# Attention and experts in one kernel: the last batch gated as a whole, gate weights and w1 in part on GpSimd, two ranks' rows in one product

## The chip, the cores and the metric

One core of a Trainium2 chip runs the kernel. The metric is the device time of one execution in microseconds, lower is better; the time before is a median of three runs, 620.59 us (620.38 to 622.92).

## The reference

Eight batches of 576 tokens go through attention with eight heads of 64 (four with a local mask of 32 positions, four with a strided one). The result, 4608 tokens of 512 values, goes through a layer of eight experts: each token is sent to the one expert with the largest logit.

```python
def _moe_ref(x, w_gate, w_output_gate, w1, w2):
    logits = x @ w_gate                                  # 4608 x 8
    e_idx = np.argmax(logits, axis=1)
    probs = softmax(logits); gate_w = probs[np.arange(N), e_idx]
    eom = 1.0 / (1.0 + np.exp(-(x @ w_output_gate)))
    for e in range(E):
        mask = e_idx == e
        h = np.maximum(x[mask] @ w1[e], 0.0)             # 512 -> 1024
        ye = h @ w2[e]                                   # 1024 -> 512
        out[mask] = gate_w[mask, None] * eom[mask, e, None] * ye
```

## The kernel before

**Order.** Both halves of the kernel stand under a manual schedule: each engine executes its instructions in the order in which the program writes them, and waits only for data. So the order of the Python calls is the order of every queue.

**Attention** (line 173) walks over 40 steps, five per batch, with the stages of several steps interleaved. Beside them run generators, the chains: each `pump()` advances those that are due, and a `yield n` puts a chain off by n pumps. A chain `logits` (line 409) computes the logits of half a batch: eight products on TensorE, a copy to `lg` on ScalarE, three turns (transposes) on TensorE, a sum on VectorE; then it goes on into `gating` (line 539). After step 40 a second loop drains the pipeline; from its fourth pass on it only pumps chains and calls `fill`.

**Gating** of n blocks of 96 tokens: one-hot `oh` of the chosen expert (VectorE), `numbers` (TensorE: running number of each token in its expert, from the counts `cum` so far), `slots` (VectorE), then `hit`, which compares the slot's low and high part with constant rows, and `named`, five products of the high part with the token's number (two) and with three bf16 parts of its gate weight (`parted`). `place(v0, v1)` (line 658) multiplies `hit` and `named` of all blocks held on TensorE and `enter` adds the result to `book`, which lists for every expert its tokens and weights. Batches 0 to 6 are gated whole (HALVED = 7); batch 7 in two halves of three blocks, its numbers going through `cum` one after the other. For the very last half `place(0, 2)` comes first, so that `tokens_first` can work out `idx0`, the rows of the leading expert; `weights`, `parted` and the other three `named` follow on VectorE, then `count` and `place(2, 5)`.

**Fillers.** The expert with the most tokens in the first four batches leads (rank 0). Its first 256 rows go through the first layer while attention still runs: `lead_layer` (line 500) yields one product at a time, 32 in all, and `fill(n)` (line 746) issues n of them, two instructions each. Eight products make a pair of columns j; the four pairs alternate between two PSUM banks of `acc`. When a pair is finished, `flush` evacuates it: `hha` by a ScalarE activation, then `hla` by a VectorE operation (lines 509, 510). While `hold[0]` is set a finished pair stays, until a later call finds `hold` cleared, or its bank is wanted two pairs later:

```python
if done and (not hold[0] or (i == c == 0 and done[0][0].start < j - 2)):
    flush(j)
```

**Experts** (line 1222). float32 operands are split into a high and a low part (`split`, line 973: a ScalarE cast, then a VectorE subtraction), and each product is three products (`w1h xh`, `w1h xl`, `w1l xh`). Rank 0 first finishes layer 2 for its first 256 rows: two groups of 24 products (`by_token`), the second interleaved with turning rank 0's other 480 rows and splitting w1. Then for each rank r: eight times `layer1(r, j)`, then `layer2`, which is interleaved with turns and splits for rank r + 1. Capacities are fixed per rank, `CAPS = (736, 704, 672, 640, 608, 576, 544, 512)`. `halves(r)` gives layer 1 one product, if at most 512 rows are left, or else two: 256 rows from `xs[0]` and the rest from `xs[1]`, into one of four PSUM banks `hps` in turn (`rotate`). The last product's width depends on the data: `choose` branches on TensorE by the spare of the rank (capacity minus tokens) and takes n - 24 a columns, a = 0 to 3. `arms(r)` (line 1216) loads the spare into a register of TensorE. `copied` (line 964), called after `layer1(0, 1)`, makes twelve small products of `pages` into `hps[3]`.

Of the kernel before, what the change touches and what calls it, by code (L numbers as in the profile page):

```python
# [35 lines left out]
HALVED = B - 1  # L36
# [5 lines left out]
FD = (0, 1, 1)  # L42
PN = 4
LF = (5, 7)
# [16 lines left out]
def attn_moe_kernel(  # L61
# [111 lines left out]
    def attention():  # L173
        with ExitStack() as actx:
# [234 lines left out]
            def logits(b, hf):  # L409
# [129 lines left out]
            def gating(b, j0, j1, ci):  # L539
                n = j1 - j0  # L540
                steady = ci < HALVED - 1
# [34 lines left out]

                def sigmoid():
                    nc.scalar.activation(out=f[:, 4, :], in_=f[:, 3, :], func=AF.Exp, scale=-1.0)
# [25 lines left out]
                else:  # L604
# [8 lines left out]
                    exp_sum()  # L613
                    yield 0
                V.tensor_tensor(out=cum[0:QB, ci + 1, :], in0=cum[0:QB, ci, :], in1=s8, op=ALU.add)  # L615
                yield 0 if steady else 1
                dst = slots[:, tcols]
                V.tensor_tensor(out=dd[:, 3], in0=pv.rearrange("p (j e) -> p j e", j=n), in1=oh, op=ALU.mult)
                yield 0
                with nc.allow_low_precision(reason="one slot's number among zeros, written as an integer"):  # L620
                    R(out=dst, in_=dd[:, 3], axis=AX.X, op=ALU.add)
                yield 0
# [10 lines left out]
                P, last = nc.gpsimd, ci == NC - 2  # L633
# [12 lines left out]
                def parted():  # L646
                    left = wall[:, tcols]
                    for i in range(WP):
                        W.tensor_copy(out=parts[:, i, :], in_=left)
                        if i + 1 < WP:  # L650
                            W.tensor_tensor(out=rest[:, i, :], in0=left, in1=parts[:, i, :], op=ALU.subtract)
# [6 lines left out]
                def place(v0, v1):  # L658
                    wp = ps_g.tile([128, 512], F32, name="gp")[:, 0:(v1 - v0) * nh]
                    blocks = [(h[:, j, 0:128], m[:, j, v0:v1, :]) for h, m, k in held for j in range(k)]  # L660
                    for i, (h, m) in enumerate(blocks):
                        nc.tensor.matmul(out=wp, lhsT=h, rhs=m.rearrange("p v s -> p (v s)"),
                                         start=(i == 0), stop=(i == len(blocks) - 1))
                    return wp

                def enter(wp, v0, v1):
                    flat = book[:, v0:v1].rearrange("p v e k -> p (v e k)")
                    if ci:
                        V.tensor_tensor(out=flat, in0=flat, in1=wp, op=ALU.add)
                    else:  # L670
                        V.tensor_copy(out=flat, in_=wp)

                if ci == HALVED - 1:
                    yield 4
# [29 lines left out]
                else:  # L704
# [3 lines left out]
                    if held and not last:  # L708
                        wp = place(0, 2 + WP)
                        held.clear()  # L710
                        yield 1
                        enter(wp, 0, 2 + WP)
# [9 lines left out]
                    else:  # L722
                        hold[0] = True
                        fill(LF[0])
                        wp = place(0, 2)
                        enter(wp, 0, 2)
# [5 lines left out]
                        parted()  # L732
                        for v in range(2, 2 + WP):
                            name(v)
# [130 lines left out]
            while t < ns + 4 or chains or fillers:  # L865
# [20 lines left out]
                fill(FT[0][k] if k < 4 else FD[0])  # L886
# [566 lines left out]
```

## Time and profile before

| | |
|---|---|
| median of three runs | 620.59 us |
| the profiled execution | 622.88 us |
| its span, first to last instruction | 621.1 us |
| TensorE busy | 582.6 us (94%) |
| VectorE, ScalarE, GpSimd busy | 317.8, 281.1, 198.5 us |
| granted TensorE clock, mean | 0.991 |

The page cuts the span into 40 slices of 15.5 us; attention fills roughly the first eleven, the experts the rest. The timeline lists instructions in order of time with start and length, equal neighbours merged, and in brackets the idle time of the engine before them and what ended it. Ends of matmuls are modelled, and a matmul's length is longer than the distance to the next one; the distance of two starts is what a matmul costs in a row of them.

### The profile page before, as it was taken

The numbers are of one execution on the slowest core, as the hardware profiler recorded it, in microseconds if no ns is written. First come the engines' busy times: TensorE is split into PE (matmuls) and PEld (weight loads), VectorE is DVE, ScalarE is ACT, GpSimd is POOL, SyncE is SP. The second block draws the span as 40 slices with busy tenths as digits, with TensorE's granted clock in tenths as the row PEclk, the third lists the DMA queues.
The fourth block names the chain that finished last, engine by engine and source line by source line (L and its number), as shares of the span: only waits on it lengthen the run. The fifth ranks groups of instructions, "written<-read, shape, count | busy, mean of one in ns | idle before, by whom it ended". The sixth has DMA issues, their size and how long they took to land. (4 is left out here: it accounts for less than half of the span.)

```text
span 621.1 us, 14987 instructions
## 1 busy us (share of the span) xinstructions
PE 582.6 (94%) x5863; PEld 499.6 (80%) x5863; DVE 317.8 (51%) x746; ACT 281.1 (45%) x567; POOL 198.5 (32%) x285
## 2 busy tenths in 40 slices
PE   7799999988979999999999999999999999999990
PEld 5676677766657989988998899889889989988880
DVE  4888888997788353432343234235434433542400
ACT  3788777766344253333332334334334434443310
POOL 3337767666333225021401130223034034011030
PEclk9999999999999999999999999999999999999996
DMA  9898898894524755053306330642165165060010
GB/s 316 294 315 288 295 289 284 292 301 138 181 63 147 278 165 159 2 193 134 121 2 204 130 109 2 195 156 80 49 200 158 27 219 154 32 237 34 3 43 17
DMA packets 42489, 97.95 MB, mean 158 GB/s; under 512 B 5458, under 2 KB 16346, under 8 KB 42394
## 3 DMA queue, kind: packets, MB, share of 16 engines
q1 hardware_dynamic: 34122, 73.47, 36.3%
q0 software_dynamic: 6864, 19.74, 9.7%
q10 hardware_dynamic: 1408, 3.38, 1.5%
q8 instruction: 72, 1.18, 0.8%
q14 instruction: 23, 0.19, 0.1%
HBM read 77.74 MB, written 20.58 MB: 158 GB/s over the span
## 5 line engine op out<-in xcount | busy, mean ns | idle before, releaser
L1040 PE MATMUL hp<-xh,w1h 128*128 128x256 f32 (+2 forms) x448 | 138.2, 308 | 0.2 <-issue 0.2
L1040 PE MATMUL hp<-xl,w1h 128*128 128x256 f32 (+2 forms) x448 | 138.0, 308 | 0.1
L1040 PE MATMUL hp<-xh,w1l 128*128 128x256 f32 (+2 forms) x448 | 137.9, 308 | 0.0
L1040 PEld LDWEIGHTS hp<-xl,w1h 128*128 128x128 f32 x448 | 84.8, 189 | 1.5 <-DVE xl L975 0.4
L1040 PEld LDWEIGHTS hp<-xh,w1h 128*128 128x128 f32 x448 | 84.8, 189 | 1.5 <-DVE copies L971 0.3
L1040 PEld LDWEIGHTS hp<-xh,w1l 128*128 128x128 f32 x448 | 84.8, 189 | 0.5
L1153 POOL DMA_INDIRECT out_dram<-ys,idx x32 | 32.9, 1027 | 133.2 <-ACT ys L1152 128.8
L1055 DVE SCALAR_TENSOR_TENSOR hlb<-hp,hhb 128x384 fp32r<-128x384 f32 (+4 forms) x64 | 35.0, 549 | 78.6 <-ACT hf L1054 78.6
L1153 POOL DMA_INDIRECT out_dram<-ys,ri x18 | 20.0, 1113 | 172.2 <-ACT ys L1152 169.1
L1052 ACT ACTIVATE hhb<-hp 128x384 fp32r<-128x384 f32 (+4 forms) x64 | 31.0, 484 | 95.5 <-PE hp L1040 94.0
L1066 PE MATMUL yp<-w2h,hhb 128*128 128x512 f32 (+1 forms) x176 | 70.3, 400 | 0.0
L975 DVE TENSOR_TENSOR xl<-tp,xh 128x512 fp32r<-128x512 f32 (+3 forms) x40 | 25.8, 649 | 86.9 <-ACT xh L974 86.9
L1066 PE MATMUL yp<-w2l,hhb 128*128 128x512 f32 (+1 forms) x176 | 68.7, 391 | 0.0
L1066 PE MATMUL yp<-w2h,hlb 128*128 128x512 f32 (+1 forms) x176 | 68.6, 390 | 0.0
L974 ACT CAST xh<-tp 128x512 fp32r<-128x512 f32 (+3 forms) x40 | 22.0, 556 | 101.1 <-PE tp L1028 101.1
L309 POOL TENSOR_TENSOR p_t<-p_t,st 128x512 f32<-128x512 f32 x40 | 42.6, 1064 | 53.5 <-DVE cum L615 15.8
L158 POOL DMA_INDIRECT xg<-xd,idx x40 | 43.5, 1088 | 15.1 <-issue 8.2
L1066 PE MATMUL yp<-w2h,hha 128*128 128x512 f32 x112 | 45.3, 405 | 2.2 <-ACT w2h L974 1.6
L975 DVE TENSOR_TENSOR w1l<-raw,w1h 128x1024 fp32r<-128x1024 f32 x32 | 39.1, 1224 | 12.2 <-ACT w1h L974 12.0
L1152 ACT ACTIVATE ys<-yp,pages 128x512 f32<-128x512 f32 (+1 forms) x36 | 24.9, 693 | 45.0 <-issue 35.5
L1066 PE MATMUL yp<-w2l,hha 128*128 128x512 f32 x112 | 43.9, 392 | 0.5 <-DVE w2l L975 0.5
L1066 PE MATMUL yp<-w2h,hla 128*128 128x512 f32 x112 | 43.7, 390 | 0.0
(214 smaller groups left out, 1096.2 us busy)
## 6 DMA issues: line engine op xcount, KB each, us to landing
raw<-in_moe_w_dram SPq DMA_DIRECT2D x54, 512.0 KB
vst<-in_vs_dram SPq DMA_DIRECT2D x8, 780.0 KB
vlt<-in_vl_dram SPq DMA_DIRECT2D x16, 292.5 KB
q_t<-in_ql_dram SPq DMA_DIRECT2D x8, 576.0 KB
q_t<-in_qs_dram SPq DMA_DIRECT2D x7, 650.0 KB
xd<-x_t SPq DMA_DIRECT2D x80, 54.0 KB
xd<-x_t SPq DMA_DIRECT2D x16, 256.0 KB
raw<-in_moe_w_dram ACTq DMA_DIRECT2D x6, 512.0 KB
```

Source lines behind the costliest of these rows:

```text
L158: nc.gpsimd.indirect_dma_start(out=dst, out_offset=None, in_=src, in_offset=bass.IndirectOffsetOnAxis(ap=idx, axis=0), bounds_check=top, o ...
L309: nc.gpsimd.tensor_tensor(out=p_t, in0=p_t, in1=st, op=ALU.subtract)
L974: nc.scalar.copy(out=hi, in_=src)
L975: nc.vector.tensor_tensor(out=lo, in0=src, in1=f32(hi), op=ALU.subtract)
L1040: nc.tensor.matmul(out=hp[:, 0:n], lhsT=w[:, k, 128 * j:128 * (j + 1)], rhs=x[:, k, 0:n], start=first, stop=(k == KC - 1 and w is w1l))
L1052: nc.scalar.activation(out=hh[:, j, 0:s], in_=hp[:, 0:s], func=AF.Relu)
L1055: nc.vector.scalar_tensor_tensor(out=hl[:, j, 0:s], in0=hp[:, 0:s], scalar=0.0, in1=f32(hh[:, j, 0:s]), op0=ALU.max, op1=ALU.subtract)
L1066: nc.tensor.matmul(out=yp[0:m, :], lhsT=h[:, j, o:o + m], rhs=w[:, j, :], start=(j == 0 and q == 0), stop=(j == FC - 1 and q == 2))
L1152: nc.scalar.activation(out=ys[0:m, 0:n], in_=yp[0:m, 0:n], func=AF.Copy, scale=w[0:m, :])
L1153: i = nc.gpsimd.indirect_dma_start(out=out.rearrange("t (k d) -> (t k) d", k=k), out_offset=bass.IndirectOffsetOnAxis(ap=row, axis=0), in_ ...
```

## The change

- Batch 7 is gated as a whole, six blocks (HALVED = 8). The chain of its second half sets `hold` right after its logits and issues three fillers; four more come before `numbers`. Batch 6's placing moves behind `numbers`; the slots come next, and counts and the sum of exponentials later. `hold` is cleared after `count_on`. The drain loop issues no fillers while a chain runs; 4 + 11 stand around the two placings.
- `parted` of batch 7 runs on GpSimd, as that of the others did; its `named` stay on VectorE.
- In the drain loop's first four passes the norms come ahead of the three pumps, not between them.
- In `experts`, the four memsets of `hps` become ScalarE activations; `arms(0)` moves from between the two groups of layer 2 into the second, at j = 5; the low parts of w1's last two chunks are subtracted on GpSimd; `first_spare` writes its integer with one instruction fewer; `copied` is called after `layer1(0, 3)`.
- Ranks whose rows exceed 512 by at most 64 (5 and 6: 576 and 544) take their first 512 rows from `xs[1]` as one product, the others from `xs[0]`. If the spare covers those others, only the first product is issued, 576 - 24 a or 544 - 24 a columns wide.

```diff
-HALVED = B - 1
+HALVED = B
+STEADY = B - 2
-FD = (0, 1, 1)
-LF = (5, 7)
+LF = (4, 11, 4, 3)
@@ logits
+                if b == B - 1 and hf:
+                    hold[0] = True
+                    fill(LF[3])
                 yield 1
@@ gating
                     sigmoid()
+                    if last:
+                        fill(LF[2])
                     pv = numbers()
-                    counts()
+                    if last:
+                        before = place(0, 2 + WP)
+                        held.clear()
+                        own_number()
+                        slot()
+                    else:
+                        counts()
...
                         if i + 1 < WP:
-                            W.tensor_tensor(out=rest[:, i, :], in0=left, in1=parts[:, i, :], op=ALU.subtract)
+                            P.tensor_tensor(out=rest[:, i, :], in0=left, in1=parts[:, i, :], op=ALU.subtract)
...
-                    if held and not last:
-                        wp = place(0, 2 + WP)
-                        held.clear()
-                        yield 1
-                        enter(wp, 0, 2 + WP)
                     for v in range(2):
                         name(v)
...
-                        hold[0] = True
                         fill(LF[0])
                         wp = place(0, 2)
+                        enter(before, 0, 2 + WP)
+                        exp_sum()
                         enter(wp, 0, 2)
                         for _ in tokens_first(0, HB, idx0):
                             pass
-                        hold[0] = False
                         for _ in weights():
                             pass
                         parted()
+                        counts()
+                        count_on()
+                        hold[0] = False
                         for v in range(2, 2 + WP):
                             name(v)
                         fill(LF[1])
@@ drain loop
                 for part in range(3):
                     at(norm, 4, part)
-                    if k < PN:
-                        pump()
                 at(rows, 4)
+                for _ in range(3 if k < PN else 0):
+                    pump()
...
-                fill(FT[2][k] if k < 4 else FD[2])
+                fill(FT[2][k] if k < 4 else 0 if chains else 4)
@@ experts
+    def over(r):
+        return rows_of(r) - WXB if 0 < rows_of(r) - WXB <= 64 else 0
...
+    def layer1_over(r, j):
+        m, n = over(r), rows_of(r)
+        (hp, rest), (hh, hl) = (rotate(hps) for _ in range(2)), hs[1]
+        a0 = -(-m // STEP) - 1
+        def form(a):
+            if a == a0:
+                products(rest, xs[0], j, m)
+            products(hp, xs[1], j, WXB if a == a0 else n - STEP * a)
+        choose(arms(r), a0, a0 + ARMS, form)
+        nc.scalar.activation(out=hh[:, j, :], in_=hp, func=AF.Relu)
+        nc.scalar.activation(out=hf[:, j, 0:m], in_=rest[:, 0:m], func=AF.Relu)
+        nc.vector.scalar_tensor_tensor(out=hl[:, j, :], in0=hp, scalar=0.0, in1=f32(hh[:, j, :]), op0=ALU.max, op1=ALU.subtract)
...
         for hp in hps:
-            nc.vector.memset(hp[:, WB - STEP * (ARMS - 1):WXB], 0.0)
+            nc.scalar.activation(out=hp[:, WB - STEP * (ARMS - 1):WXB], func=AF.Copy, scale=0.0,
+                                 in_=ecst[:, 0, 0:1].to_broadcast([128, WXB - WB + STEP * (ARMS - 1)]))
...
-        arms(0)
         between = {j: [(turn, 0, c, m)] for j, (c, m) in zip(TURN_AT, blocks(0))}
+        between[5] = [(arms, 0)]
         for c in range(2, KC):
-            between[TURN_AT[c - 2]].append((split_w, 0, 1, c))
+            between[TURN_AT[c - 2]].append((split_w, 0, 1, c, nc.gpsimd))
...
                     count_spare()
                     send_away()
+                if r == 0 and j == 3:
                     copied()
```

## Rows read from the trace of the kernel before

**Rows 1.** The page's slices of the span: busy tenths of TensorE

```profile
PE   7799999988979999999999999999999999999990
```

**Rows 2.** Timeline of TensorE, 161 to 187 us: start, length, operation, idle time before

```profile
161.40 0.69 PE L416 MATMUL gp<-xt,wgt 128*32 128x288 f32 x8
...
171.94 0.29 PE L662 MATMUL gp<-named,hit 96*128 96x96 bf16 x3 [1.70 <-DVE named L656]
172.07 3.25 PE L525 MATMUL sp<-xe,raw 128*128 128x256 f32 x14
...
176.20 0.35 PE L662 MATMUL gp<-named,hit 96*128 96x144 bf16 x3 [0.66 <-DVE named L656]
...
179.51 0.50 PE L1066 MATMUL yp<-w2h,hha 128*128 128x512 f32 x1 [1.62 <-ACT w2h L974]
...
186.69 0.49 PE L1066 MATMUL yp<-w2h,hha 128*128 128x512 f32 x1 [0.60 <-DVE hp L1231]
```

**Rows 3.** Timeline of VectorE, 169 to 177 us, the last half batch

```profile
169.89 0.15 DVE L618 TENSOR_TENSOR dd<-gp,oh 96x24 f32<-96x24 f32 x1
...
171.37 0.52 DVE L656 TENSOR_TENSOR named<-hit,hcst 96x144 bf16<-96x144 bf16 x2
...
172.27 0.25 DVE L669 TENSOR_TENSOR book<-book,gp 128x96 f32<-128x96 f32 x1 [0.38 <-PE gp L662]
...
175.34 0.80 DVE L656 TENSOR_TENSOR named<-hit,parts 96x144 bf16<-96x144 bf16 x3
...
176.07 0.68 DVE L510 SCALAR_TENSOR_TENSOR hla<-sp,hha 128x512 fp32r<-128x512 f32 x1
```

**Rows 4.** Timeline of ScalarE at 173 us, the third pair of the lead layer

```profile
173.20 0.60 ACT L509 ACTIVATE hha<-sp 128x512 fp32r<-128x512 f32 x1 [5.20 <-PE sp L525]
```

**Rows 5.** Timeline of VectorE and GpSimd, batch 6 with its six blocks

```profile
156.51 0.95 DVE L706 TENSOR_TENSOR hit<-hcst,lo 96x768 bf16<-96x768 f32 x1
...
159.16 0.18 POOL L649 CAST parts<-wall 96x6 bf16<-96x6 f32 x1
...
160.20 0.19 POOL L649 CAST parts<-rest 96x6 bf16<-96x6 f32 x1
```

**Rows 6.** Timeline of TensorE and VectorE, layer 1 of rank 0

```profile
199.76 0.69 PE L970 MATMUL hp<-pages,ident 128*64 128x96 f32 x12 [0.63 <-DVE pages L959]
...
207.19 0.35 PE L1040 MATMUL hp<-xh,w1l 128*128 128x408 f32 x1
...
208.29 0.66 DVE L1055 SCALAR_TENSOR_TENSOR hlb<-hp,hhb 128x480 fp32r<-128x480 f32 x1 [1.56 <-ACT hf L1054]
```

**Rows 7.** Timeline of VectorE, TensorE and GpSimd, and from the page a GpSimd group

```profile
192.20 1.22 DVE L975 TENSOR_TENSOR w1l<-raw,w1h 128x1024 fp32r<-128x1024 f32 x1
...
196.57 0.34 PE L1040 MATMUL hp<-xh,w1l 128*128 128x408 f32 x1
...
170.56 0.59 POOL L649 CAST parts<-rest 96x3 bf16<-96x3 f32 x1
...
L309 POOL TENSOR_TENSOR p_t<-p_t,st 128x512 f32<-128x512 f32 x40 | 42.6, 1064 | 53.5 <-DVE cum L615 15.8 <-DVE st L294 13.7 <-DVE f L588 6.2
```

**Rows 8.** Line 1040 by form, ranks 5, 6, 7 (first, last start), and two products of 512

```profile
L1040 PE MATMUL hp<-xh,w1h x64: 273/280/283, 472.5 to 494.8; 128*128 128x256 f32 x32, 128*128 128x248 f32 x32
...
L1040 PE MATMUL hp<-xh,w1h x64: 272/278/287, 520.1 to 542.0; 128*128 128x256 f32 x32, 128*128 128x240 f32 x32
...
L1040 PE MATMUL hp<-xh,w1h x32: 357/362/363, 566.5 to 585.1; 128*128 128x440 f32 x32
...
470.50 0.39 PE L1066 MATMUL yp<-w2h,hhb 128*128 128x512 f32 x1
...
471.86 0.39 PE L1066 MATMUL yp<-w2h,hhb 128*128 128x512 f32 x1
```

**Rows 9.** Stretches at the end: busy of TensorE, its loads, VectorE, ScalarE, GpSimd; granted clock

```profile
606.00:610.00 4.00, 0.04 (x1) 0.00 (x0) 0.00 (x0) 0.69 (x1) 0.97 (x1) 1.00 0.17 66
610.00:612.00 2.00, 0.00 (x0) 0.00 (x0) 0.00 (x0) 0.00 (x0) 0.00 (x0) 0.52 0.00 0
```

More of the change, by code (lines that the diff above doesn't have):

```diff
@@ L575, in exp_sum, with count_on, own_number, slot @@
                     R(out=f[:, 2, :], in_=dd[:, 1], axis=AX.X, op=ALU.add)
+                last = ci == NC - 2
+                dst = slots[:, tcols]
+                def count_on():
+                    V.tensor_tensor(out=cum[0:QB, ci + 1, :], in0=cum[0:QB, ci, :], in1=s8, op=ALU.add)
+                def own_number():
+                    V.tensor_tensor(out=dd[:, 3], in0=pv.rearrange("p (j e) -> p j e", j=n), in1=oh, op=ALU.mult)
+                def slot():
+                    with nc.allow_low_precision(reason="one slot's number among zeros, written as an integer"):
+                        R(out=dst, in_=dd[:, 3], axis=AX.X, op=ALU.add)
+                def place(v0, v1):
+                    wp = ps_g.tile([128, 512], F32, name="gp")[:, 0:(v1 - v0) * E * HB]
+                    blocks = [(h[:, j, 0:128], m[:, j, v0:v1, :]) for h, m, k in held for j in range(k)]
+                    for i, (h, m) in enumerate(blocks):
+                        nc.tensor.matmul(out=wp, lhsT=h, rhs=m.rearrange("p v s -> p (v s)"),
+                                         start=(i == 0), stop=(i == len(blocks) - 1))
+                    return wp
+                def enter(wp, v0, v1):
+                    flat = book[:, v0:v1].rearrange("p v e k -> p (v e k)")
+                    if ci:
+                        V.tensor_tensor(out=flat, in0=flat, in1=wp, op=ALU.add)
+                    else:
+                        V.tensor_copy(out=flat, in_=wp)
                 def sigmoid():
@@ L609, in gating @@
                     sigmoid()
+                    if last:
+                        fill(LF[2])
                     pv = numbers()
-                    counts()
+                    if last:
[3 more added lines that the diff above has]
+                        slot()
+                    else:
+                        counts()
+                        yield 0
+                        exp_sum()
+                        yield 0
+                if not last:
+                    count_on()
+                    yield 0 if steady else 1
+                    own_number()
                     yield 0
-                    exp_sum()
+                    slot()
                     yield 0
[L615 to L622, printed above, removed]
                 def weights():
@@ L631, in weights @@
                     yield 0
-                P, last = nc.gpsimd, ci == NC - 2
+                P = nc.gpsimd
                 W = V if last else P
@@ L656, in name @@
                     W.tensor_tensor(out=named[:, :, v, :], in0=high, in1=wide(val, nh), op=ALU.mult)
[L658 to L673, printed above, removed]
+                if ci == STEADY:
                     yield 4
@@ L732, in gating @@
                         parted()
+                        counts()
+                        count_on()
+                        hold[0] = False
                         for v in range(2, 2 + WP):
@@ L986, in place @@
     def place(r, c):
+        if over(r):
+            return (1, 128 * c) if 128 * c < WXB else (0, 0)
         return (1, 128 * c) if alone(r) else (0, 128 * c) if 128 * c < EH else (1, 128 * c - EH)
@@ L1012, in gather, with split_w @@
             xgs[r, c] = xg
-    def split_w(r, which, c):
+    def split_w(r, which, c, eng=nc.vector):
         raw = raws[r, which, c]
         if which == 1:
-            split(w1h[:, c, :], w1l[:, c, :], raw)
+            split(w1h[:, c, :], w1l[:, c, :], raw, eng)
         else:
```

40 lines of the change are left out of this document (22 added, 18 removed).

## The prediction

> **What bounds the kernel now.** I read the page's slices first. TensorE is busy in nine tenths or more of nearly every slice; after the start it dips a little in the ninth and tenth, and most in the twelfth, 171 to 186 us [rows 1], where attention hands over to the experts. From there to the end it never rests, so behind it only work that leaves TensorE counts, and inside it the waits. The timeline of TensorE alone gives those waits [rows 2]: 1.70 us at 171.94 and 0.66 at 176.20 (it waits for VectorE's `named`), 1.62 at 179.51 (for the cast of w2 on ScalarE), 0.60 at 186.69. All four can be reached by this change. The run profiled took 622.88 us with a span of 621.1; the median is 620.59. I sum differences inside the profiled execution and apply them to the median.
>
> **Part 1, the last batch gated in one chain.** The number of fillers (products of the lead layer, line 525) stays 32: ten by FT in both kernels, then 22 that now stand at fixed places, 3 + 4 + 4 + 11 by LF. One filler is two instructions, 14 of them took 3.25 us [rows 2], so 0.46 us each. The other products are the same but for one set of running numbers instead of two (some 0.2 us). What changes is the order, and I follow it from the last logits at 161.40 [rows 2].
>
> Up to the first placing, TensorE has the logits (0.5), 13 fillers (6.0), two sets of turns (0.6), the numbers (0.3) and batch 6's placing (0.6): it stands before `place(0, 2)` at 169.5. VectorE needs the numbers, which come at about 167.3 (after 9 of the fillers). For three blocks it then took from 169.89 to the end of `named` at 171.89, 2.0 us [rows 3]; for six the broad comparison takes 0.95 us [rows 5], where three take about half, so 2.8 for all: 170.1. The wait is 0.5 us (0 to 1.2) where it was 1.70.
>
> Next stands the step I think decides. `hold` is now set at the last logits, so the second pair of the lead layer (fillers 9 to 16) ends while it holds and isn't evacuated. Its evacuation is written out at filler 22, the first of the 11, and its VectorE half therefore queues behind what was written before it: both `enter`, `tokens_first`, `weights`, `counts`, `count_on` and three `name`. Filler 25 opens the fourth pair in the same PSUM bank and has to wait for it. The kernel before shows how such an evacuation queues: ScalarE's half of the third pair ran at 173.20 [rows 4], VectorE's only at 176.07, right behind the three `named` of 175.34 [rows 3]. There it cost nothing, as the second pair had been evacuated long before.
>
> The price: `place(0, 2)` from 170.1 (0.3), fillers 22 to 24 (1.4): TensorE is free at 171.8. VectorE does `enter` of batch 6 and the sum from 170.1 (0.6), then the chain that went before from `enter` at 172.27 to the end of the evacuation at 176.75, 4.5 us [rows 3]. The parts move to GpSimd: 1.2 us for five instructions, 159.16 to 160.39 [rows 5], against as much on VectorE before, but counts and the first names now run beside them; six blocks add 0.1 to each name. I take 4.35 (4.1 to 4.9), so 175.05, and a **new wait of 3.3 us** (2.8 to 4.1).
>
> Then 8 fillers (3.7) bring TensorE to 178.8. `count` and `place(2, 5)` find their names ready: the 0.66 goes. ScalarE again casts w2 only behind the last evacuation, so the 1.62 stays [rows 2] and the first product of layer 2 comes at about 180.5 where it was 179.51. The low half of w2 queues behind the last evacuation, `cnt` and `enter`, 0.2 more. Part 1: **+1.2 us** (-0.3 to +2.5), in spite of 1.9 us of waits removed.
>
> Other queues: GpSimd has the five parts ahead of the four gathers of rank 0. They start at about 174.0 as before, after idx0, and are wanted only 14 us later. The norms moved ahead of the pumps touch VectorE alone and hide in batch 7's products; 0 (-0.2 to +0.2).
>
> **Part 2, `arms(0)` into the second group of layer 2.** The register load on TensorE stood where 0.60 us of waiting is shown [rows 2], named as the memset of `hp` just behind the value that it loads. At j = 5, some 5 us after that value, I expect no wait: **-0.6** (-0.7 to 0). The four memsets go to ScalarE, which has idled from the w1 casts to `ys`: 1 us hidden there.
>
> **Part 3, `copied` from j = 1 to j = 3.** It writes hps[3], and j = 3 is the product that has just written hps[3]. Before, it waited 0.63 us for `pages` [rows 6]. Now it must wait until that product is evacuated: at j = 4 the product's last matmul ended at 207.54 and VectorE at 208.95 [rows 6], 1.4 us. So **+0.8** (+0.4 to +1.0).
>
> **Part 4, half of w1's low parts on GpSimd.** VectorE takes 1.22 us for 1024 columns; GpSimd's nearest two-input float product took 1.06 for 512 [rows 7], so about 2.1. VectorE's second part ran from 192.20 to 193.42; two parts at 0.9 us more each end at 195.2. Layer 1 wants the last of them with its twelfth product, at 196.57 [rows 7], and both shift together with the stage: 1.3 us of cover, 0 (0 to +1 if they stretch). VectorE's relief is worth nothing either: the last `xl` waits for its ScalarE half. On the Trainium skill's page GPSIMD Engine Reference, section Key points, GpSimd shares its SBUF interfaces with VectorE and contends with VectorE instructions that have two SBUF inputs. The cast at 170.56 took 0.59 us where the like at 159.16 took 0.18, while such a comparison ran on VectorE [rows 5, 7]; that agrees. By that rule the parts of part 1 could stretch by 0.4 us each time, which the upper end 4.9 already holds.
>
> **Part 5, one product of 512 rows for ranks 5 and 6.** The widths show the spare: 256 + 248 of 576 means a spare of 72 or more, 256 + 240 of 544 means 48 to 71 [rows 8]. In both cases the new choice leaves the extra columns out: 504 and 496 columns (480, if rank 5's spare were 96 or more; rank 6's 473 to 496 rows leave that open, and I take 504). Now rank 5's 192 products start 0.118 apart (22.3 us over 189 intervals), 22.6 in all; rank 6's 22.2. A start interval at 440 columns is 0.200, at 512 it is 0.227 (six in 1.36 us) [rows 8]. For 504 I get 0.223 from the second row and 0.228 from the line through 252 and 440; 96 of them are 21.4 to 21.9. For 496: 21.1 to 21.5. **-1.75** for both (-1.3 to -2.2), straight on the path, since TensorE has no idle time there. The first product now needs four turned blocks, not two; the turns stand ahead of the last group of layer 2, 5 us of products, so 0.
>
> **Sum:** +1.2 - 0.6 + 0.8 - 1.75 = -0.35. Forecast **620.3 us**, its own range 618.4 to 622.2 from the ends above.
>
> **Rivals.** *The wait at filler 25 isn't there*, because VectorE reaches the evacuation by the time TensorE has done filler 24. Then part 1 is about -2.1: 617.0. For it: 4.35 is a sum of many short instructions. Against: the queue order is written out, and [rows 3] show an evacuation held behind the names. 22%.
>
> *The wait slows TensorE's clock.* The place is again filler 25, the longest pause of TensorE after the first 10 us. At the end of the kernel the granted clock was still 1.00 from 606 to 610, with TensorE at rest but for 0.04 us, and 0.52 from 610 to 612 [rows 9]; a pause of 3.3 is inside that, one of 4 isn't surely. If it falls to half, the eight fillers behind cost 3.7 us more, and with the first products of layer 2 some 5: 624 to 625.5, slower than before. [...] 8%. The Trainium skill, TensorE: Matmul & The Clock Gate, section What's actually happening, says that idleness throttles the array and activity releases it; the end of this trace agrees on the first.
>
> *The wide product gains nothing*, because the start interval of a wide product, or the evacuation of 512 columns behind it, grows as much as the second product saves. 622.0. Against: 64 columns more than the 440 form that runs without idle time. 10%.
>
> **How the numbers follow.** The forecast 60%, the three rivals 22, 8 and 10. About 0.5% (3.1 us) is what a measurement of this kernel can tell from no change, so faster means under 617.5. The first rival lies around that line and its better half beyond; with a tail of the forecast I give faster 0.25, slower 0.08 (the clock), same 0.67. The range 615.9 to 622.8 leaves out the clock and the best tenth.
>
> **What would show it.** In TensorE's timeline: a wait of about 3.3 us before a filler, released by VectorE's `hla` (line 510), three fillers after the 96-column placing; no wait before `place(2, 5)`; first product of layer 2 about 1 us later; no wait before the second group; 1.4 us before the twelve products on `pages`, released by `hlb`. Among the forms of layer 1: 504 and 496 columns, 96 each, rank 5's stage 1 us shorter. Wrong would be a first product of layer 2 before 178.5, or rank 5 as long as before.

## The result, and the profile after

The changed kernel takes 624.76 us (median of five runs), the kernel before 620.59 beside it: a ratio of 1.0053 over all runs, 95% interval 1.003 to 1.0075. It is slower by 3.3 us (1.9 to 4.7; the two medians alone stand 4.2 apart), where 620.3 with a range up to 622.8 was forecast. The profiled execution took 624.76 us with a span of 622.5.

The slices of TensorE and of its granted clock (40 slices of 15.6 us, tenths), from the page of the changed kernel, answer to [rows 1]:

```profile
PE   8898999899849999999999999999999999999990
...
PEclk9999999999979999999999999999999999999996
```

The dip in the twelfth slice is deeper than before (4 where it was 7), and the clock dips with it. Nothing else stands out, so I go to that slice, the handover from attention to the experts. TensorE's timeline of the changed kernel (start, length, operation, idle time before it and what ended it) answers to [rows 2]; fillers are now line 528, placings 597, layer 2 is 1112:

```profile
159.30 0.69 PE L416 MATMUL gp<-xt,wgt 128*32 128x288 f32 x8
...
168.13 0.43 PE L597 MATMUL gp<-named,hit 96*128 96x96 bf16 x6 [0.65 <-DVE named L694]
168.40 1.53 PE L528 MATMUL sp<-xe,raw 128*128 128x256 f32 x6
177.35 5.57 PE L528 MATMUL sp<-xe,raw 128*128 128x256 f32 x16 [7.43 <-DVE hla L513]
...
182.79 0.54 PE L597 MATMUL gp<-named,hit 96*128 96x144 bf16 x6
184.71 0.47 PE L1112 MATMUL yp<-w2h,hha 128*128 128x512 f32 x1 [1.39 <-DVE book L604]
185.02 0.40 PE L1112 MATMUL yp<-w2h,hla 128*128 128x512 f32 x1
185.81 0.50 PE L1112 MATMUL yp<-w2l,hha 128*128 128x512 f32 x1 [0.39 <-DVE w2l L996]
```

The new wait stands where it was predicted, three fillers after the 96-column placing and released by `hla`, but it lasts 7.43 us and not 3.3. The wait before `place(0, 2)` fell from 1.70 to 0.65, and that before `place(2, 5)` is gone. The eight fillers behind the pause (16 instructions) take 5.57 us, though 14 such instructions took 3.25 in [rows 2]. VectorE's timeline of the changed kernel shows whom `hla` waited for, and answers to [rows 3]:

```profile
169.65 0.17 DVE L455 TENSOR_SCALAR idx<-tn 128x6 int32<-128x6 f32 x1
...
171.41 0.46 DVE L694 TENSOR_TENSOR named<-hit,parts 96x288 bf16<-96x288 bf16 x1 [0.79 <-POOL parts L687]
174.41 0.46 DVE L694 TENSOR_TENSOR named<-hit,parts 96x288 bf16<-96x288 bf16 x1 [2.55 <-POOL parts L687]
176.24 0.46 DVE L694 TENSOR_TENSOR named<-hit,parts 96x288 bf16<-96x288 bf16 x1 [1.38 <-POOL parts L687]
176.62 0.68 DVE L513 SCALAR_TENSOR_TENSOR hla<-sp,hha 128x512 fp32r<-128x512 f32 x1
```

VectorE itself is idle for 4.7 us ahead of the three names (0.79 + 2.55 + 1.38): each waits for a part on GpSimd. GpSimd's timeline of the changed kernel, whole from 170 to 176.3:

```profile
170.09 1.08 POOL L158 DMA_INDIRECT xg<-xd,idx  x1 [9.92 <-DVE f L665]
171.18 0.20 POOL L687 CAST parts<-wall 96x6 bf16<-96x6 f32 x1
171.54 1.21 POOL L158 DMA_INDIRECT xg<-xd,idx  x1 [0.16 <-issue]
172.78 0.20 POOL L689 TENSOR_TENSOR rest<-wall,parts 96x6 f32<-96x6 f32 x1
173.14 1.03 POOL L158 DMA_INDIRECT xg<-xd,idx  x1 [0.16 <-issue]
174.18 0.20 POOL L687 CAST parts<-rest 96x6 bf16<-96x6 f32 x1
174.54 1.19 POOL L158 DMA_INDIRECT xg<-xd,idx  x1 [0.16 <-issue]
175.76 0.21 POOL L689 TENSOR_TENSOR rest<-rest,parts 96x6 f32<-96x6 f32 x1
176.03 0.18 POOL L687 CAST parts<-rest 96x6 bf16<-96x6 f32 x1
```

The four gathers of rank 0, which `experts` issues far behind `parted` in the program's text, stand between the five parts in GpSimd's queue. The parts need 1.0 us, the issue of the four gathers 4.5. So the last part ends at 176.2 where a row of parts from 170.3, the end of `wall`, would have ended at about 171.5, by the 1.2 us of [rows 5]. The first gather starts at 170.09, before `wall` is there for the first part, so it does stand ahead of the part in the queue. That a gather holds the queue only while it is issued is seen here too: the next part starts 0.01 us behind the gather's row, while the gathers' data moves until about 177.5. The Trainium skill, Perfetto Trace Analysis, section DMA Instruction — SWDGE (GPSIMD), says that such a row ends with the descriptors and not with the data; the trace agrees.

The stretches of the changed kernel (start:end, length, busy time of TensorE, its loads, VectorE, ScalarE, GpSimd, each with its count, then the granted clock, DMA share and GB/s) show the second half of the loss:

```profile
172.00:174.00 2.00, 0.00 (x0) 0.00 (x0) 0.00 (x0) 0.00 (x0) 1.81 (x3) 1.00 0.59 152
174.00:176.00 2.00, 0.00 (x0) 0.00 (x0) 0.46 (x1) 0.00 (x0) 1.76 (x4) 0.58 0.64 211
176.00:178.00 2.00, 0.65 (x2) 0.56 (x3) 1.05 (x2) 0.60 (x1) 0.18 (x1) 0.50 0.32 115
178.00:180.00 2.00, 2.00 (x6) 1.63 (x5) 0.69 (x1) 0.00 (x0) 0.00 (x0) 0.50 0.00 0
180.00:182.00 2.00, 2.00 (x8) 1.64 (x7) 0.00 (x0) 0.00 (x0) 0.00 (x0) 0.72 0.00 0
182.00:184.00 2.00, 1.33 (x12) 0.94 (x10) 0.41 (x1) 1.04 (x2) 0.00 (x0) 1.00 0.00 0
```

TensorE rests from 169.9; at about 174.3 its clock falls to the lower level (0.50, 1.2 GHz) and at about 181.1, with the fillers running since 177.35, it comes back to 1.00. The fillers take 1.9 us more than at the full clock (3.7 us for 16 instructions by the 3.25 for 14).

Last, the ranks of one product, line 1078 by form (shortest, median, longest in ns, first and last start, form), which answer to [rows 8]:

```profile
L1078 PE MATMUL hp<-xh,w1h x32: 386/388/388, 476.5 to 497.6; 128*128 128x504 f32 x32
...
L1078 PE MATMUL hp<-xh,w1h x32: 382/382/383, 523.0 to 543.4; 128*128 128x496 f32 x32
```

504 and 496 columns as expected. From rank 5's first product to rank 6's it is 46.5 us (47.6 before), from there to rank 7's 45.2 (46.4): 2.3 us less.

### The profile page after: what moved, and what is told of

The parts are those of the page before. It is cut to its first block, busy times and chain, and to the rows that moved or that the text cites. A ratio compares the mean times of both kernels' runs of the same rounds, so it can differ in the third digit from the quotient of the medians.

```text
span 622.5 us, 14509 instructions
## 1 busy us (share of the span) xinstructions
PE 580.3 (93%) x5670; PEld 490.8 (79%) x5670; DVE 308.8 (50%) x699; ACT 278.1 (45%) x553; POOL 202.2 (32%) x282
## 5 line engine op out<-in xcount | busy, mean ns | idle before, releaser
L1078 PE MATMUL hp<-xl,w1h 128*128 128x256 f32 (+8 forms) x384 | 126.9, 330 | 0.1
L1078 PE MATMUL hp<-xh,w1h 128*128 128x256 f32 (+8 forms) x384 | 127.0, 331 | 0.0
L1078 PE MATMUL hp<-xh,w1l 128*128 128x256 f32 (+8 forms) x384 | 126.9, 330 | 0.0
L1112 PE MATMUL yp<-w2h,hhb 128*128 128x512 f32 (+1 forms) x208 | 83.2, 400 | 0.0
L1112 PE MATMUL yp<-w2l,hhb 128*128 128x512 f32 (+1 forms) x208 | 81.3, 391 | 0.0
L1101 DVE SCALAR_TENSOR_TENSOR hlb<-hp,hhb 128x384 fp32r<-128x384 f32 (+3 forms) x48 | 28.2, 590 | 68.1 <-ACT hf L1100 64.2
L1098 ACT ACTIVATE hhb<-hp 128x384 fp32r<-128x384 f32 (+3 forms) x48 | 24.9, 518 | 81.8 <-PE hp L1078 73.5
L1112 PEld LDWEIGHTS yp<-w2l,hhb 128*128 128x128 f32 (+1 forms) x208 | 38.8, 187 | 8.7
L1112 PEld LDWEIGHTS yp<-w2h,hhb 128*128 128x128 f32 (+1 forms) x208 | 38.9, 187 | 8.1 <-issue 0.4
L1112 PEld LDWEIGHTS yp<-w2h,hlb 128*128 128x128 f32 (+1 forms) x208 | 38.9, 187 | 7.7
```

Source lines behind the costliest of these rows:

```text
L1078: nc.tensor.matmul(out=hp[:, 0:n], lhsT=w[:, k, 128 * j:128 * (j + 1)], rhs=x[:, k, 0:n], start=first, stop=(k == KC - 1 and w is w1l))
L1098: nc.scalar.activation(out=hh[:, j, 0:s], in_=hp[:, 0:s], func=AF.Relu)
L1101: nc.vector.scalar_tensor_tensor(out=hl[:, j, 0:s], in0=hp[:, 0:s], scalar=0.0, in1=f32(hh[:, j, 0:s]), op0=ALU.max, op1=ALU.subtract)
L1112: nc.tensor.matmul(out=yp[0:m, :], lhsT=h[:, j, o:o + m], rhs=w[:, j, :], start=(j == 0 and q == 0), stop=(j == FC - 1 and q == 2))
```

## How the runs are read

Executions of one kernel differ by some 5 us. In the traces most of that lies ahead of the last logits: they start at 158.3 to 161.7 us in the eight traces with the new gating chain and at 159.9 to 162.8 in the four with the old one. Whether the change has a share in that, one trace of each kernel can't tell. So I read each experiment in pieces that hardly vary: from the last logits to the first product of layer 2 (A), from there to the first product of layer 1 (B), and from rank 0's first product of layer 1 to rank 1's (C). All are differences of starts in TensorE's timeline. "Clock" is the lowest that was granted between the last logits and layer 1.

| kernel | A | B | A + B | clock | C |
|---|---|---|---|---|---|
| before | 18.11 | 14.51 | 32.62 | 1.00 | 42.1 |
| changed | 25.41 | 13.43 | 38.84 | 0.50 | 41.9 |
| changed, gathers behind the parts | 21.19 | 13.42 | 34.61 | 0.50 | 42.3 |
| changed, parts on VectorE | 19.83 | 13.42 | 33.25 | 1.00 | 41.9 |
| changed, hold ended early | 20.36 | 15.01 | 35.37 | 0.50 | 42.4 |
| changed, both of these | 16.60 | 14.89 | 31.49 | 0.50 | 41.9 |
| the same, copied at j = 1 | 16.59 | 14.65 | 31.24 | 0.50 | 42.4 |
| both, and no idle TensorE | 16.59 | 13.43 | 30.02 | 1.00 | 41.8 |
| changed, busy in the pause | 28.82 | 13.43 | 42.25 | 1.00 | 44.1 |
| before, parts on GpSimd | 23.61 | 15.09 | 38.70 | 0.50 | 42.3 |
| before, one product for ranks 5, 6 | 18.11 | 14.52 | 32.63 | 1.00 | 42.2 |
| before's attention, new experts | 18.05 | 15.20 | 33.25 | 0.50 | 42.3 |

Without a fall of the clock B is 14.5 with the old experts and 13.4 with the new; a fall within it adds 0.6 to 1.8. C is some 2 us longer than usual in one row, "busy in the pause": there the wait ahead of `copied` is 2.08 us, and the clock falls once more behind it, to 0.50 from about 214.5 to 217.9 us, with products 0.34 us apart that otherwise stand 0.19 apart.

## The experiments

**The gathers behind the parts.** The theory: the parts are late because each waits behind a gather's issue. The rival: they are slow on GpSimd by themselves, or the chain of six blocks is long.

```diff
+    idx0g = const.tile([128, HB], I32, name="idx0g")
+    nc.gpsimd.memset(idx0g, 0)
...
                         parted()
+                        P.tensor_scalar(out=idx0g[0:QB, :], in0=parts[:, WP - 1, :], scalar1=0.0, scalar2=None, op0=ALU.mult)
+                        P.tensor_tensor(out=idx0g, in0=idx0g, in1=idx0, op=ALU.add)
...
-            fetch(..., idx[0:m, r, k:k + 1] if r else idx0[0:m, k:k + 1], N)
+            fetch(..., idx[0:m, r, k:k + 1] if r else idx0g[0:m, k:k + 1], N)
```

> The changed kernel, with rank 0's gathers reading a copy of idx0 that GpSimd writes behind the five parts, so that the parts no longer stand between the gathers; nothing is left out. Theory A (the parts were late because each waited behind a gather of 1.0 to 1.2 us): the five parts run in a row in about 1.2 us from 170.3, the wait at filler 25 falls from 7.43 to about 3.0 us, TensorE's granted clock stays at 1.00, the eight fillers behind it take 3.7 us instead of 5.4, the stretch from the last logits to layer 1 falls from 38.8 to about 32.8 us, and the time from 624.8 to 618.5 to 619. Theory B (the parts are slow on GpSimd by themselves, beside VectorE's work, or the chain of six blocks is long): the wait stays above 6 us and the time at 624 to 625. Theory C (gathers that start some 2 us later come too late for the turns): the wait falls as in A, but the second group of layer 2 waits for the turns, 621 to 622.

Its median is 622.19 us, a ratio of 1.0003 to the kernel before (0.9977 to 1.003). GpSimd's timeline, first and last part and first gather, and the wait in TensorE's:

```profile
171.08 0.19 POOL L689 CAST parts<-wall 96x6 bf16<-96x6 f32 x1 [10.19 <-DVE wall L670]
...
172.67 0.19 POOL L689 CAST parts<-rest 96x6 bf16<-96x6 f32 x1
...
174.60 1.10 POOL L160 DMA_INDIRECT xg<-xd,idx0g  x1 [0.87 <-POOL idx0g L754]
...
174.00 5.41 PE L530 MATMUL sp<-xe,raw 128*128 128x256 f32 x16 [3.36 <-DVE hla L515]
```

The parts take 1.8 us in a row (the two subtractions 0.46 each, beside VectorE's names) and the wait falls from 7.43 to 3.36 us, about the 3.3 of the prediction. The rival is out. The gathers start at 174.6 and B is unchanged, so the prediction was right that they aren't wanted early. One expectation missed: the clock fell behind this pause too, and the fillers took 5.41 us, so that A + B is 34.61 us for the 32.8 expected and the time 622.19 for 618.5 to 619.

**The parts on VectorE, as before.**

```diff
-                        P.tensor_copy(out=parts[:, i, :], in_=left)
+                        W.tensor_copy(out=parts[:, i, :], in_=left)
...
-                            P.tensor_tensor(out=rest[:, i, :], in0=left, ...
+                            W.tensor_tensor(out=rest[:, i, :], in0=left, ...
```

> The changed kernel with the last batch's five parts on VectorE, as in the kernel before; nothing is left out. Theory A: parts (1.2 us) and three names (1.3 us) follow one another on VectorE from 170.6, the evacuation ends at about 173.7, the wait at filler 25 is about 3.8 us (0.8 more than with the parts in a row on GpSimd), the clock stays at 1.00, 619.5. If the clock falls from a pause of about 3.8 us already, the eight fillers behind take 5 us or more and the time is 621 to 622. Theory B (chain of six blocks): wait above 6 us, 624 or more.

621.06 us, ratio 0.9997 (0.997 to 1.0023). In TensorE's timeline, and in the stretches of that kernel:

```profile
175.97 3.72 PE L528 MATMUL sp<-xe,raw 128*128 128x256 f32 x16 [3.69 <-DVE hla L513]
```

```profile
174.00:176.00 2.00, 0.03 (x1) 0.03 (x1) 1.89 (x6) 0.00 (x0) 1.70 (x2) 1.00 0.61 160
176.00:178.00 2.00, 2.00 (x9) 1.79 (x10) 0.69 (x1) 0.60 (x1) 1.18 (x2) 1.00 0.70 211
```

The wait is 3.69 us as expected, A + B 33.25, 0.6 more than before. Here the clock stayed at 1.00 and the fillers took 3.72 us, right behind the evacuation and with the gathers still moving. By the trace (+0.6 in the handover, -2.3 in ranks 5 and 6) this kernel should be 1.7 us faster than before; the interval, -1.9 to +1.4, holds that only near its end. It may be that other executions had a fall, but that was not seen.

**The hold ended early.** The theory: the wait is there because pair 2's evacuation is written behind the names.

```diff
                     else:
+                        hold[0] = False
                         fill(LF[0])
...
                         count_on()
-                        hold[0] = False
```

> The changed kernel with the hold ended ahead of the four fillers of the first fixed place, so that the second pair of the lead layer is evacuated right behind the first two names; parts stay on GpSimd between the gathers; nothing is left out. Theory A (the wait is that evacuation's place in VectorE's queue): no wait at filler 25; place(2, 5) waits instead, about 3 us, for the last name at 176.7; no fall of the clock; the first product of layer 2 comes about 6 us sooner than in the changed kernel, 618.5 to 619. Theory B (what is late is the names, and whatever waits for them takes the same pause): the pause only moves, and with the clock the gain stays under 2 us, 623 or more.

622.14 us, ratio 0.9998 (0.9979 to 1.0017). The wait at filler 25 is gone; in TensorE's timeline the pause is now here:

```profile
179.17 0.84 PE L597 MATMUL gp<-named,hit 96*128 96x144 bf16 x6 [3.87 <-DVE named L694]
```

So both theories hold a part: the place of the evacuation decides where TensorE waits, the parts decide until when. A + B is 35.37, 3.5 us better than the changed kernel and not 6: the pause was 3.87 us where about 3 was expected, and the clock fell as it ended, so that layer 2's first products ran at the lower level (B is 15.01 for 13.43).

**Both edits together.** The two diffs above in one kernel.

> The changed kernel with the hold ended early and the parts on VectorE; nothing is left out. Theory A: no wait at filler 25, place(2, 5) waits 0 to 0.5 us, from the last logits to layer 1 about 30 us (before 32.6, changed 38.8), 616 to 617, faster than both kernels. Rival: ScalarE's casts of w2 behind the last evacuation then set the first product of layer 2, with a wait of 2 us or more there: 617.5 to 618.5.

618.04 us, ratio 0.9945 (0.9909 to 0.9981): faster than both kernels. `place(2, 5)` no longer waits, A is 16.60. A + B is 31.49, not 30, as the clock fell to 0.50 from about 175.7 to 179, though no wait was longer than 1.86 us.

**The kernel before with its parts on GpSimd.** This asks whether the interleaving is a matter of the new gating chain.

```diff
-                        W.tensor_copy(out=parts[:, i, :], in_=left)
+                        P.tensor_copy(out=parts[:, i, :], in_=left)
...
-                            W.tensor_tensor(out=rest[:, i, :], in0=left, ...
+                            P.tensor_tensor(out=rest[:, i, :], in0=left, ...
```

> The kernel before with one edit: the five parts of the last half batch on GpSimd; nothing is left out. Theory A (in GpSimd's queue the parts come to stand between the four gathers of rank 0, 1.0 to 1.2 us each): idx0 is there at 173.7, the last part at about 179.7, place(2, 5) waits about 4.5 us instead of 0.66, layer 1 starts 4 us later after the last logits than the 32.6 of the kernel before, 5.7 if TensorE's clock falls in the pause. Theory B (the parts run in a row, 1.2 us, and only the six-block chain of the change made them late): the wait stays under 1.5 us, the stretch 32.5 to 33.5.

628.31 us, ratio 1.0101 (1.0067 to 1.0135). GpSimd's timeline, the first of four such pairs, and TensorE's:

```profile
173.91 1.07 POOL L158 DMA_INDIRECT xg<-xd,idx  x1 [1.06 <-DVE f L627]
174.99 0.20 POOL L649 CAST parts<-wall 96x3 bf16<-96x3 f32 x1
175.34 1.08 POOL L158 DMA_INDIRECT xg<-xd,idx  x1 [0.15 <-issue]
...
180.12 0.52 PE L662 MATMUL gp<-named,hit 96*128 96x144 bf16 x3 [4.68 <-DVE named L656]
```

(Two runs.) The same alternation, a wait of 4.68 us where it was 0.66, and the clock falls. A + B grows by 6.1 us, as much as by the whole change. That one edit is enough.

**TensorE busy in the pause.** The changed kernel, with products that nobody reads ahead of filler 25.

```diff
-                        fill(LF[1])
+                        fill(3)
+                        warm = ps_g.tile([128, 512], F32, name="gp")
+                        for _ in range(30):
+                            nc.tensor.matmul(out=warm[:, 0:256], lhsT=raws[0, 1, 0][:, 0:128], rhs=xe[:, 0, :],
+                                             start=True, stop=True)
+                        fill(LF[1] - 3)
```

> The changed kernel with 30 more products of 256 columns into a bank that nobody reads, ahead of filler 25, so that TensorE works through the 7.4 us in which it waits for VectorE; nothing is left out. Clock theory (the eight fillers behind the wait took 5.4 us and not 3.7 because the granted clock was 0.50 behind the pause): the evacuation ends at the same point, the wait shrinks to under 1 us, the granted clock stays at 1.00, the fillers take 3.7 us, and from the last logits to layer 1 it is 37.1 us instead of 38.8. Rival (they took longer for their operands or for the gathers beside them): 5.4 us still, 38.8.

629.61 us, ratio 1.0122 (1.0086 to 1.0158), from two runs. I had counted one instruction for a product where there are two, so the 30 products lasted 13 us and not 7, and TensorE came to filler 25 at 182.9, some 5.4 us after the evacuation had ended. The total therefore says nothing. What the run was for can still be read: the granted clock stayed at 1.00, and the eight fillers behind took 3.62 us, against 5.57. In the changed kernel the gathers' data had also landed by 177.5, as the fillers began. Here the operands had lain ready for 5.4 us; with the parts on VectorE they had not, the gathers were still moving, and at 1.00 the fillers took 3.72. So it was the clock, not the fillers' operands or the gathers.

**One product for ranks 5 and 6 alone.** The kernel before with `over`, `layer1_over` and the placing of blocks that belongs to them.

```diff
     def place(r, c):
+        if over(r):
+            return (1, 128 * c) if 128 * c < WXB else (0, 0)
...
     def layer1(r, j):
+        if over(r):
+            layer1_over(r, j)
+            return
```

> The kernel before with part 5 alone, ranks 5 and 6 in one product; nothing is left out. By the prediction -1.75 us (ratio 0.9972); by the stages of the changed kernel's trace -2.3 us (1.1 and 1.2), ratio 0.9963. If part of those 2.3 belongs to the other edits, less than 1.5.

619.29 us, ratio 0.9947 (0.9929 to 0.9965), that is -3.3 us (-2.2 to -4.4). By the trace ranks 5 and 6 take 46.5 and 45.3 us, 2.2 less than before, and A + B and C are those of the kernel before; those 2.2 lie at the near end of the interval, and if the gain is larger, its source isn't shown. The whole gain that the trace shows in the ranks belongs to this part.

**The attention of before with the new experts.** Parts 2 to 5 without part 1; of its diff the lines that [rows 2, 6, 7] bear on:

```diff
-        arms(0)
         between = {j: [(turn, 0, c, m)] for j, (c, m) in zip(TURN_AT, blocks(0))}
+        between[5] = [(arms, 0)]
         for c in range(2, KC):
-            between[TURN_AT[c - 2]].append((split_w, 0, 1, c))
+            between[TURN_AT[c - 2]].append((split_w, 0, 1, c, nc.gpsimd))
...
                     send_away()
+                if r == 0 and j == 3:
                     copied()
```

> The attention of the kernel before with all of the change behind it (parts 2 to 5: the register load later, memsets on ScalarE, two low parts of w1 on GpSimd, copied at j = 3, one product for ranks 5 and 6); nothing is left out. By the traces: part 2 -0.6, parts 3 and 4 nothing (rank 0's stage took 41.9 where it took 42.1), part 5 -2.3, in all -2.9 us (ratio 0.9953). By the prediction, with +0.8 for copied: -1.55 (0.9975). If the relief in the handover is taken up by the next wait there: -2.3.

619.93 us, ratio 0.9959 (0.9939 to 0.998), -2.5 us (-1.2 to -3.8). The waits of A are those of before (1.70, 0.59, 1.62); yet in its stretches the clock fell, in the middle of layer 2, with TensorE at work:

```profile
182.00:184.00 2.00, 1.95 (x7) 1.59 (x8) 2.00 (x2) 2.00 (x5) 0.00 (x0) 0.78 0.12 47
184.00:186.00 2.00, 2.00 (x6) 1.57 (x5) 1.91 (x5) 2.00 (x4) 0.00 (x0) 0.50 0.00 0
```

That took away what the later register load gives, in this execution.

**`copied` back at j = 1, on top of the two edits.**

```diff
                 if r == 0 and j == 1:
                     count_spare()
                     send_away()
-                if r == 0 and j == 3:
                     copied()
```

> The changed kernel with the hold ended early, the parts on VectorE and copied back at j = 1; nothing is left out. If the wait for hlb at j = 3 (1.47 us in the changed kernel) costs what the prediction said, rank 0's stage falls from 41.9 us to about 41.1 and the time is 0.8 us below that of the kernel with the first two edits. If the wait is made up for inside the stage (41.9 in the changed kernel, 42.1 in the kernel before), the stage stays at 41.9 to 42.2 and the time the same: about 618 where the kernel before is at 621.5 (ratio 0.9945).

617.05 us, ratio 0.9914 (0.9884 to 0.9943). C is 42.4 where the kernel with both edits has 41.9: the wait for `pages` there is 1.25 us, that for `hlb` at j = 3 was 1.47, and neither place is better by what these runs can tell. The interval overlaps that of both edits, too.

**No idle TensorE behind the last placing**, again on top of the two edits.

```diff
                         enter(place(2, 2 + WP), 2, 2 + WP)
+                        idle = ps_t.tile([128, 2, 2, 128], F32, name="tp").rearrange("p a b n -> p (a b n)")
+                        for _ in range(3):
+                            nc.tensor.matmul(out=idle[:, 0:256], lhsT=raws[0, 1, 0][:, 0:128], rhs=xe[:, 0, :],
+                                             start=True, stop=True)
```

> The changed kernel with the hold ended early, the parts on VectorE and three products of 256 columns into a bank that nobody reads, behind place(2, 5), where TensorE waits 1.9 us for VectorE; nothing is left out. Clock theory: the granted clock stays at 1.00 through the handover, the first products of layer 2 stand 0.23 us apart and not 0.43, and from the last logits to layer 1 it is 30.0 us where the kernel without the three products showed 31.5 with a fall. Rival (the fall comes all the same, or the three products delay the first product of layer 2): 31.5 or more.

616.57 us, ratio 0.9916 (0.9887 to 0.9944). A + B is 30.02 us as expected. TensorE's timeline and the stretches:

```profile
176.09 0.47 PE L1116 MATMUL yp<-w2h,hha 128*128 128x512 f32 x1 [0.51 <-DVE book L604]
```

```profile
176.00:178.00 2.00, 1.52 (x6) 0.98 (x7) 2.00 (x2) 2.00 (x3) 0.00 (x0) 1.00 0.53 170
178.00:180.00 2.00, 2.00 (x10) 1.67 (x9) 2.00 (x3) 2.00 (x6) 0.00 (x0) 1.00 0.00 0
```

Work that nobody uses, put where TensorE would rest, doesn't delay A by anything (16.59 both times), and the clock stayed at 1.00 in the execution that was profiled. That the products kept it there is argued, not shown: it stayed at 1.00 without them in the kernel before and behind the 3.69 us with the parts on VectorE, and one trace of each kernel is all there is. In the times this kernel and the one with `copied` back can't be told apart; both are some 5 us faster than the kernel before.

## Why the prediction was wrong

**The step that failed** is the last of part 1: "GpSimd has the five parts ahead of the four gathers of rank 0." That was the order of the program's text, taken for that of the queue: the section on the kernel before says that the order of the Python calls is the order of every queue, and GpSimd's rows show that here it is not. The parts are written in `attention()`, the gathers in `experts()`, each under a manual schedule of its own; parts and gathers keep their own order, but the queue mixes the two. No row of the kernel before showed it, since there the last parts ran on VectorE. I priced the parts with the row of batch 6, where no gather was near [rows 5], and put the rival order neither into the range nor among the rivals. Its price was in reach, in a group of the page of the kernel before (busy time, mean ns of one):

```profile
L158 POOL DMA_INDIRECT xg<-xd,idx x40 | 43.5, 1088 | 15.1 <-issue 8.2
```

Four gathers of 1.09 us, behind an index that comes before the weights do, make the wait 3.3 + 4.4 = 7.7 us; it was 7.43. Why the queue is laid out in this order no run shows; it came out so in every kernel with these parts on GpSimd, except where the gathers were made to depend on the parts.

**Part 1 otherwise.** The wait at filler 25, its cause and its place were right, and with the parts in a row it is 3.36 us (GpSimd) or 3.69 (VectorE) for 3.3 forecast. The 1.62 ahead of layer 2, said to stay, came out at 1.39. A grew by 7.3 us where part 1 had +1.2: +4.1 for the longer wait and +1.9 for the clock make that 7.2. The waits that went, 1.70 to 0.65 and 0.66 to nothing, are those of the prediction.

**The clock** was a rival at 8%, of the right place and sign: "If it falls to half, the eight fillers behind cost 3.7 us more". They cost 1.9, because it came back while they ran. That the measured 624.76 lies in this rival's 624 to 625.5 is luck: the rival had some 5 us from the clock alone, and the runs show 1.9 from it and 4.1 from a longer wait that the rival did not have. Its condition, that a pause of 3.3 us is safe and one of 4 not surely, is refuted in both directions: no fall behind 3.69 us, one behind 3.36, and in three kernels one behind waits of at most 1.9. The end of the kernel [rows 9] was one sample, and I read a limit out of it.

**Part 2**, -0.6 forecast: B shrank by 1.1 us. In the kernel before, the products on both sides of the register load start 0.99 us apart, at 186.69 [rows 2] and here in the same timeline:

```profile
185.70 0.39 PE L1066 MATMUL yp<-w2l,hha 128*128 128x512 f32 x1
```

Their neighbours stand 0.23 apart, so the load cost 0.76 and not only the 0.60 shown as waiting; the low half of w2 gave 0.13, the rest is in small pieces. No run has this part alone at the full clock, so the shares are read from the starts and not measured apart.

**Part 3**, +0.8 forecast: nothing. The wait was sized right (1.4 forecast), as TensorE's timeline of the changed kernel shows:

```profile
209.16 0.69 PE L991 MATMUL hp<-pages,ident 128*64 128x96 f32 x12 [1.47 <-DVE hlb L1101]
```

But the stage as a whole did not get longer: C is 41.8 to 42.4 with `copied` at either place, the row with the busy pause left out. Before, the wait it replaces was 0.63 us [rows 6], with both edits and `copied` back 1.25. The starts in the traces tell where the difference went: from the last product of rank 0's layer 1 to rank 1's first it is 21.4 us (start to start) in all eight traces with `copied` at j = 3, and 21.9 to 22.2 in the four with it at j = 1. So half a microsecond came back behind layer 1; why, isn't shown.

**Part 4**, 0 forecast: 2.4 us for each low part on GpSimd instead of 2.1, and hidden: the second ended at 199.35, and no product waited for it.

**Part 5**, -1.75 forecast: -2.2 to -2.3. The mechanism was right. The forecast's own terms (22.6 and 22.2 before; 21.65 and 21.3, the middles, behind) give -1.85, so 0.1 of the miss is arithmetic. For 504 columns I had taken 0.223 to 0.228 per product; the row gives 21.1 us for 93 intervals, 0.227. For 496 it is 20.4 us, 0.219. 96 products each make 21.8 and 21.1 us, at or inside the ends that I had for each, and 1.9 less than before; the other 0.3 to 0.4 lies outside the products, where I had counted nothing and have no row for it.

**The sum** with the measured terms: +7.3 - 1.1 + 0 + 0 - 2.3 = +3.9 us, for the 3.3 (1.9 to 4.7) of the ratio. The spans of the two traces differ by 1.4 only, as the changed kernel's last logits came 2.1 us sooner in its trace, which is not in the sum. The ends of the forecast's terms, simply added, run from 617.6 to 624.0 us; how its own range of 618.4 to 622.2 was drawn from them isn't said. The gain in the experts was larger than forecast, and five small instructions moved to another queue cost almost twice as much.

## What to carry to other kernels

When small instructions on a critical chain move to another engine, look up what that engine's queue holds at that moment, and price both orders: an indirect gather holds GpSimd's queue for 1.0 to 1.2 us, and five instructions of 0.2 us became a chain of 6.1. Where a pause of TensorE can't be avoided, count the clock behind it as 1 to 2 us (1.2 to 2.1 in the seven traces in which it fell in this handover) that may or may not come. Products that nobody reads, put into the pause, went with a clock of 1.00 in the handover in both traces that have them. The two small edits that the study points to, evacuating ahead of the pause and leaving the parts on VectorE, make the rest of the change worth 3.4 us; the two kernels built on them came out at some 5, one with the idle time filled and one without, so filling isn't shown to add to it.

## What the runs showed of the hardware

- The clock of TensorE does not follow the length of the last pause alone. The kernel before and the one with its attention and the new experts have the same waits ahead of layer 2 (1.70, 0.6, 1.62 us); the one kept 1.00, the other fell to 0.50 at about 183.1, with TensorE at work without rest since 182.05, and came back at about 186.5. The Trainium skill, TensorE: Matmul & The Clock Gate, section What's actually happening, says that the monitor runs freely and is not restarted by the kernel, so that the same work can meet it at another phase; these two runs fit that, but do not show it. What decides in a single execution was not found.
- A subtraction of 1024 float columns took 2.4 us on GpSimd and 1.2 on VectorE. While it ran on GpSimd, an instruction of VectorE of 8 columns at 198.59 took 0.78 us, and ended with it (199.37 and 199.35); in the kernel before, with nothing on GpSimd beside it, the same instruction took 0.16. GpSimd's and VectorE's timelines of the changed kernel, then VectorE's of the kernel before:

```profile
194.60 4.75 POOL L996 TENSOR_TENSOR w1l<-raw,w1h 128x1024 fp32r<-128x1024 f32 x2 [0.81 <-ACT w1h L995]
...
198.59 0.78 DVE L954 SCALAR_TENSOR_TENSOR rk<-cnt,ecst 128x8 f32<-128x8 f32 x1
...
194.47 0.16 DVE L933 SCALAR_TENSOR_TENSOR rk<-cnt,ecst 128x8 f32<-128x8 f32 x1
```

- A part of six columns on GpSimd took 0.18 to 0.21 us between gathers; in a row beside VectorE's names the two subtractions among the five took 0.46, each beginning inside a name and ending 0.05 us or so behind it.
